# A fixed order of the items of every engine in place of a list scheduler's, and key sums by vector passes that transpose blocks

## The chip, the cores and the metric

The kernel runs on one core of a Trainium2 chip. The metric is the device time of one execution in microseconds (us); the time given for a kernel is the median of several runs. One execution is also taken by the hardware profiler, and all rows below are from that one.

## What is computed

For 64 heads (8 batches of 8) with 576 tokens of 64 channels, a linear attention with 256 features per token, and behind it a feed forward over all 4608 tokens:

```python
def phi(x):
    proj = x @ w_phi                                   # 64 -> 128
    proj = proj - max(abs(proj), axis=-1)
    return concat([exp(proj), exp(-proj)])             # 256 features
q_p, k_p = phi(q), phi(k)
kv  = k_p^T @ v                                        # 256 x 64 per head
z   = sum(k_p, over the tokens)                        # the key sums, 256 per head
out = (q_p @ kv) / (q_p @ z + 1e-6)
x   = out as 4608 x 512
y   = (max(x @ w_in, 0) ** 2) @ w_out                  # 512 -> 2048 -> 512
```

## The kernel before, in words

Two heads make a *pair*; there are 32 pairs, four of them per batch. The feed forward runs in 18 *chunks* of 256 tokens (c0 to c17), each in 8 *steps* (f0 to f7) of 256 hidden columns. A step is a first product (`gemm1`, L1051, 24 f16 matmuls into one PSUM bank `ph`), a scale and squares on ACT and DVE, and a second product (`gemm2`, L1088, 12 matmuls that add up in PSUM over the eight steps). Chunks c0 to c9 run so; the last eight run as four pairs of chunks with a saving scheme (L1233, "p1" and "p2", two parts of a first product for both chunks). The weights arrive as 64-bit words and are rebuilt on the chip: per block a load of 1 MB (L464), a size on ACT (L480), a low part on POOL (L483), a join on DVE (L487), a greatest value on ACT (L502, input weights only), a scale that PE spreads over the partitions (L422) and DVE rounds (L428 to L433), and two halves (L551 or L552, then L555) or three parts (L521, L331, L541).

The first six pairs are *early* (`early`): PE does all their work with transposes and sums of its own (k products L611 and L617, key times value L669, L674, key sums L702, turning L714, q products L730, L736, L764, L768, numerators L783, denominators L800). The other 26 pairs are *late* (`visit`, `late`): a visit is one block of PE work for three pairs at once (q products L884, then the next pair's k products L611, then columns L892, L617, L669, L674, then the last pair's numerators L904); POOL finds the greatest q projections (L982) and sums the denominators (L1003). In `keys` the late pairs' key features are folded by DVE adds (L650, L655, L660 over both heads) into one row, and in `late` that row is transposed in blocks of 32 x 32 (L966) and reduced (L967); it goes to DRAM and back (L971, L972) and is summed once more (L974). Tokens end in the `ring`, from which the feed forward reads (a multiply L835, a high part L857 or L864, a low part L860).

Nothing is issued while these lines run. Each is added as an item to a `Plan`: its engine (some have a second engine to choose), an assumed time, what it comes after and which buffers it uses. `order` is a list scheduler: it plays the items by assumed times, takes on each engine the ready item with the lowest rank (1108 ranks are set one by one, `RANKS`, read in `improve`), and returns them by start. They are then issued in that order, so each engine's stream is fixed when the program is built. Where the played PE stands idle for over 0.7 us before 125 us, matmuls of zeros (L1358) are put in.

Of the kernel before, what the change touches and what calls it, by code (L numbers as in the profile page):

```python
# [27 lines left out]
F = 128  # L28
# [21 lines left out]
STAY = 6.0  # L50
LATER = 2.0
BEHIND = 0.0
MOVED = 70.0
# [32 lines left out]
class Plan:  # L86
# [24 lines left out]
    def close(self):  # L111
# [18 lines left out]

        for (tag, n), mine in users.items():
            if tag in self.single:
                first = mine[0]
                first.after += [a for op in mine[1:] for a in op.after if a not in mine and not self.leads(first, a)]
        self.users = {key: len(mine) for key, mine in users.items()}

    def leads(self, first, op):
        seen, todo = set(), [op]
        while todo:
            x = todo.pop()  # L140
            if x is first:
                return True
            for a in x.after:
                if a.n not in seen:
                    seen.add(a.n)
                    todo.append(a)
        return False

    def improve(self):

        some = [op for op in self.ops if -50.0 < op.rank < MOVED]
        assert 2 * len(some) == len(RANKS)
        for n, op in enumerate(some):
            i, j = (DIGITS.index(x) for x in RANKS[2 * n:2 * n + 2])
            op.rank = (90 * i + j - 3000) * 0.05
        return self.order()

    def order(self):
        for op in self.ops:
            op.start = op.end = None  # L160
            op.next, op.left = [], 0
            op.after = [a for a in {id(a): a for a in op.after}.values() if a is not op]
            op.behind = [a for a in op.behind if a not in op.after and a is not op]
        for op in self.ops:
            for a in op.after + op.behind:
                a.next.append(op)
                op.left += 1
        free = dict.fromkeys(self.HOP, 0.0)
        waiting = {e: [] for e in self.HOP}
        ready = {e: [] for e in self.HOP}  # L170
        holder, open_at, parked = {}, {}, {}
# [3 lines left out]

        def alone(op):
            return [key for key in op.uses if key[0] in self.single]

        def release(op):
            least = max([open_at.get(tag, 0.0) for tag, n in alone(op) if holder.get(tag) != n] + [a.start + 0.001 for a in op.behind], default=0.0)  # L180
            for eng in op.ways:
                at = least
                for a in op.after:
                    at = max(at, a.there + (self.HOP[a.eng] if a.eng != eng or a.land else 0.0))
                second = eng != next(iter(op.ways))
                heapq.heappush(waiting[eng], (at + LATER * second, op.rank + BEHIND * second, op.n))

        def gone(n):
            return self.ops[n].start is not None

        for op in self.ops:
            if not op.left:
                release(op)
        done = 0
        while done < len(self.ops):
            best = None
            for e in self.HOP:
                while ready[e] and gone(ready[e][0][1]):
                    heapq.heappop(ready[e])
                while waiting[e] and gone(waiting[e][0][2]):  # L200
                    heapq.heappop(waiting[e])
                if not waiting[e] and not ready[e]:
                    continue
                t = free[e] if ready[e] else max(free[e], waiting[e][0][0])
                if best is None or t < best[0]:
                    best = t, e
# [42 lines left out]
            for x in op.next:  # L249
                x.left -= 1  # L250
                if not x.left:
                    release(x)
# [1189 lines left out]
```

## Time and profile before

| what | us |
|---|---|
| median of 3 runs (1019.26 to 1021.61) | 1020.16 |
| span of the profiled execution | 1018.5 |
| PE busy | 999.8 |
| DVE busy | 763.2 |
| ACT busy | 680.5 |
| POOL busy | 361.2 |

The span runs from the first to the last instruction; the runs' median lies 1.7 us above it. PE's granted clock was 0.998 of full speed over the span. PE's busy time counts matmuls, with those of zeros among them; weight loads are counted apart (694.6 us) and mostly lie beside the matmuls. A busy PE is not always a PE with useful work: a matmul's record includes its way through the array.

### The profile page before, as it was taken

How to read it: one execution, taken by the hardware profiler on the slowest of the kernel's cores; microseconds unless marked ns; L12 is line 12 of the kernel's file. 1: busy time of each engine (PE TensorE's matmuls, PEld its weight loads, DVE VectorE, ACT ScalarE, POOL GpSimd, SP SyncE). 2: the span in 40 equal slices, each digit the busy share in tenths (PEclk: the TensorE clock that was granted, in tenths of full speed). 3: DMA queues.
4: the chain of work that ended last, by engine and by line, in shares of the span. 5: the costliest groups of instructions: out<-in, count | busy, mean ns of one | idle time of the engine just before them, and what ended most of it. 6: DMA issues, size and time to landing. Idle time of an engine off the chain costs nothing.

```text
span 1018.5 us, 19261 instructions
## 1 busy us (share of the span) xinstructions
PE 999.8 (98%) x7632; PEld 694.6 (68%) x7713; DVE 763.2 (75%) x1221; ACT 680.5 (67%) x1206; POOL 361.2 (35%) x138
## 2 busy tenths in 40 slices
PE   8999999999999999999999999999999999999998
PEld 4657776776666667666767666666776767677675
DVE  5899878798878989777879888798888447343432
ACT  6989886777777787686777867776555445435444
POOL 2433356364456555475375646563000000000000
PEclk9999999999999999999999999999999999999999
DMA  9754323132322233233324212110002001000001
GB/s 355 282 186 135 122 81 94 39 110 73 85 60 81 75 93 93 60 82 81 107 80 111 83 48 69 41 41 22 13 2 83 1 1 49 14 1 21 22 1 42
DMA packets 94914, 77.34 MB, mean 76 GB/s; under 512 B 58088, under 2 KB 72424, under 8 KB 92776
## 3 DMA queue, kind: packets, MB, share of 16 engines
q1 hardware_dynamic: 94536, 75.59, 24.6%
q8 instruction: 60, 0.98, 0.4%
q10 hardware_dynamic: 288, 0.52, 0.1%
q14 instruction: 30, 0.25, 0.1%
HBM read 61.16 MB, written 14.78 MB: 75 GB/s over the span
## 4 chain that ended last, share of the span: by engine, by line
PE 90%; DVE 3%; DMA 3%; ACT 2%; issue 1%; SPq 0%; DVEq 0%; ACTq 0%
PE po L1088 27%; PE ph L1051 21%; PE pp L1233 7%; PE pz L669 4%; PE pv L1088 4%; PE pn L1088 4%; PE ph L1233 3%; PE pn L904 3%; PE pn L884 2%; PE pp L611 2%; PE pv L904 2%; PE pz L1233 2%; PE pz L674 1%; PE pv L669 1%; PE pz L892 1%
## 5 line engine op out<-in xcount | busy, mean ns | idle before, releaser
L1051 PE MATMUL ph<-ring,win 128*128 128x256 f16 x2064 | 240.4, 273 | 0.8 <-ACT r L1060 0.8
L1051 PEld LDWEIGHTS <-win 128*128 128x128 f16 x2064 | 195.3, 98 | 47.0 <-issue 24.8
L982 POOL PARTITION_ALL_REDUCE mx<-pt x52 | 121.6, 2339 | 122.7 <-ACT pt L335 84.3
L1088 PE MATMUL po<-wh,gh 128*128 128x512 f32 x448 | 143.8, 442 | 0.0
L1003 POOL PARTITION_ALL_REDUCE rb<-rb x26 | 96.5, 3712 | 112.0 <-DVE rb L1000 95.6
L1265 ACT ACTIVATE qe<-qe,cw 128x512 f32<-128x512 f32 x58 | 41.4, 715 | 112.5 <-DVE qe L1248 112.5
L1088 PE MATMUL po<-wl,gl 128*128 128x512 bf16 x448 | 115.1, 379 | 0.0
L331 DVE TENSOR_TENSOR gl<-r,gh 128x512 bf16<-128x512 f32 x86 | 87.5, 1018 | 31.7 <-ACT r L1070 30.7
L1003 POOL PARTITION_ALL_REDUCE ds<-ds x26 | 98.7, 3797 | 25.2 <-DVE ds L1000 24.5
L1088 PE MATMUL po<-wl,gh 128*128 128x512 bf16 x375 | 101.5, 379 | 4.9 <-issue 1.6
L1088 PEld LDWEIGHTS <-gl 128*128 128x128 bf16 x576 | 56.4, 98 | 68.0
L1088 PEld LDWEIGHTS po<-wh,gh 128*128 128x128 f32 x448 | 84.6, 189 | 25.9
L1248 DVE TENSOR_TENSOR qe<-pp,qe 128x512 f32<-128x512 f32 (+1 forms) x87 | 52.3, 602 | 61.3 <-PE pp L1233 59.5
L1060 ACT ACTIVATE r<-ph,cw 128x512 f32<-128x512 f32 x86 | 58.7, 683 | 51.0 <-PE ph L1051 49.3
L331 DVE TENSOR_TENSOR gl<-qe,gh 128x512 bf16<-128x512 f32 x58 | 40.1, 691 | 65.7 <-ACT qe L1070 65.6
L1088 PEld LDWEIGHTS <-gh 128*128 128x128 bf16 x576 | 52.3, 98 | 50.7 <-issue 8.9
L633 ACT ACTIVATE e<-e 128x512 f32<-128x512 f32 x64 | 40.0, 625 | 32.3 <-DVE e L630 32.3
L1233 PEld LDWEIGHTS <-win 128*128 128x128 f16 x522 | 48.8, 98 | 14.2 <-issue 7.8
L1068 ACT ACTIVATE gh<-r 128x512 fp32r<-128x512 f32 x86 | 54.1, 629 | 5.7 <-PE pv L1088 2.0
L1070 ACT ACTIVATE r<-r 128x512 f32<-128x512 f32 x86 | 54.3, 631 | 2.7
L650 DVE TENSOR_TENSOR es<-e 128x512 f32<-128x512 f32 x52 | 46.3, 890 | 4.5 <-ACT e L635 4.3
L669 PE MATMUL pz<-e,v 128*64 128x256 f32 x416 | 49.3, 379 | 0.0
(286 smaller groups left out, 1970.4 us busy)
## 6 DMA issues: line engine op xcount, KB each, us to landing
v<-in_vp_dram SPq DMA_DIRECT2D x32, 320.0 KB, 4.1
k<-in_kp_dram SPq DMA_DIRECT2D x32, 288.0 KB, 4.1
q<-in_qp_dram SPq DMA_DIRECT2D x32, 288.0 KB, 3.4
rb<-rd SPq DMA_DIRECT2D x64, 144.0 KB, 3.1
out_dram<-o SPq DMA_DIRECT2D x34, 256.0 KB, 2.1
td<-kvs SPq DMA_DIRECT2D x26, 128.0 KB, 2.6
kz<-td SPq DMA_DIRECT2D x26, 128.0 KB, 2.9
spill<-ring SPq DMA_DIRECT2D x6, 256.0 KB, 2.9
```

The lines of the kernel that those rows point to most:

```text
L331: eng.tensor_tensor(out=out_, in0=a, in1=b_, op=ALU.subtract)
L669: PE.matmul(out=to[64 * h:64 * h + 64, 0:256], lhsT=v_[p][:, t, h, :], rhs=e_[2 * p + h][:, t].rearrange("p s f -> p (s f)"), start=t == 0 ...
L904: PE.matmul(out=to[64 * h:64 * h + 64, :], lhsT=kz_[n][:, 128 * s_ + 64 * h:128 * s_ + 64 * h + 64], rhs=qe_[2 * n + h].rearrange("p (s x) ...
L982: o = P.add("POOL", par_us(S), lambda n=n, h=h: G.partition_all_reduce(mx_[n], pt_[p][:, h, :], channels=128, reduce_op=bass_isa.ReduceOp. ...
L1003: o = P.add("POOL", 3.6, lambda y=y: G.partition_all_reduce(y(), y(), channels=128, reduce_op=bass_isa.ReduceOp.add), [o], [home], R(RQ + ...
L1051: PE.matmul(out=ph[:, j, :], lhsT=win[w][:, t, 128 * ff:128 * ff + 128], rhs=at_ring(c, x, t), start=k == 0, stop=k == 3 * KT - 1)
L1060: o = P.add("ACT", act_us(512, 1), lambda: A.activation(out=r_[n], in_=ph_[bank], func=AF.Relu, scale=cw[:, f, 0:1]), [g1], [("ph", bank), ...
L1068: sq = P.add("ACT", act_us(512), lambda: A.activation(out=gh_[n], in_=r(), func=AF.Square), after, use + [("gh", n)], Q)
L1070: o = P.add("ACT", act_us(512), lambda: A.activation(out=r(), in_=r(), func=AF.Square), [sq], use, Q, other=[("DVE", 0.70, lambda: V.tenso ...
L1088: PE.matmul(out=bank(i), lhsT=x[:, j, 128 * i:128 * i + 128], rhs=w[:, j, :], start=turn + j + s == 0, stop=(turn, j, s) == (NFP - 1, 1, 2))
L1233: PE.matmul(out=to, lhsT=fl(x, *al)(k), rhs=fr(y, *ar)(k), start=n == 0, stop=n == 5)
L1248: V.tensor_tensor(out=to, in0=a, in1=b, op=ALU.add)
```

## The change

Four things change.

1. `order` no longer schedules. A text `ORDER` holds two characters for each of the 3139 items: the item's place in one list for all engines. A text `WAYS` holds one digit for each of the 558 items that may run on more than one engine: which one. The items are issued in that order. The assumed times (some of them edited) still decide where zeros are put in and nothing else. `RANKS` and `improve` go.
2. The late pairs' key sums: per head one DVE reduce over the whole 128 x 1024 features that transposes blocks of 32 x 32 on its way, and one of 128 x 256 for the tail, 3 passes per pair. Before there were 8 (three adds for each head, one transpose, one reduce). The result is 128 x 72 numbers rather than 128 x 16; it goes to DRAM and comes back by two DMAs rather than one, into columns 256 to 327 of `kz`.
3. In a visit the q products and the k products are items of their own and wait only for their own inputs; before they were one item that waited for the inputs of all three pairs, and columns and numerators waited likewise. The order may now put other work between them.
4. A second half of `close` goes, which had made the first user of a PSUM bank wait for the inputs of its later users.

The matmuls, the passes of the feed forward and the loads are the same in kind and number.

```diff
 class Plan:
     def order(self):
+        assert 2 * len(self.ops) == len(ORDER)
+        place = {}
+            i, j = (DIGITS.index(x) for x in ORDER[2 * op.n:2 * op.n + 2])
+            place[op.n] = 90 * i + j
+        several = [op for op in self.ops if len(op.ways) > 1]
+        for op, way in zip(several, WAYS, strict=True):
+            op.take(list(op.ways)[int(way)])
+        order = sorted(self.ops, key=lambda op: place[op.n])
 ...
-        return sorted(self.ops, key=lambda op: (op.start, op.n))
+        return order
 ...
     def keys(p, main, to, use, tail, to_tail, use_tail, rank):
-            o = P.add("DVE", dve_us(512), lambda n=n: V.tensor_tensor(
-                out=es_[p][:, 512:1024], in0=e_[n][:, 0:2].rearrange("p t s f -> p (t s f)"),
-                in1=e_[n][:, 2:4].rearrange("p t s f -> p (t s f)"), op=ALU.add),
 ...
+            def fold(src, col, k, after, use, rank):
+                sums[p].append(P.add("DVE", dve_us(256 * k), lambda: V.tensor_reduce(
+                    out=col(), in_=src().rearrange("p k (b x) -> p k b x", x=32), op=ALU.add, axis=AX.X, apply_transpose=True),
+                    [after], [use, ("z4", p)], rank))
 ...
     def visit(i):
+        if s is not None:
+            v.append(P.add("PE", 0.92, rows_q, [q_load[s]], [qn, qv, ("q", s)], R(0.0), mode=ROWS))
+        if k is not None:
+            v.append(P.add("PE", 0.92, rows_k, [k_load[k]], [pp, ("k", k)], R(0.0), mode=ROWS))
+        if v:
+            c = P.add("PE", us_c, columns, need, use_c, R(0.0), mode=COLS)
 ...
-            v3 = visited[0] = P.add("PE", 1.94, numerators, need + [c] + pt_of.get(s, [])[:2], use_n, R(0.0), mode=COLS)
+            v3 = visited[0] = P.add("PE", 2.04, numerators, [kz_of[n]] + qexp[n], use_n, R(0.0), mode=COLS)
 ...
     def late(p):
-        o = P.add("DVE", dve_us(512), lambda: V.transpose(es_[p][:, 512:1024], es_[p][:, 0:512]), sums[p], [("es", p)], R(RZ))
 ...
+        w = P.add("SP", 0.4, lambda: SP.dma_start(zd_[p], z4_[p]), sums[p], [("z4", p), ("zd", p)], R(RZ), land=1.9, xfer=0.1)
+        back.append(P.add("SP", 0.5, lambda: SP.dma_start(
+            kz_[p][:, 256:320].rearrange("p (a x) -> p a x", a=4),
+            zd_[p].rearrange("(a i) b x -> (i b) a x", a=4)[:, :, 0:16]), [w], [("zd", p), ("kz", p)], R(RZ), land=2.1, xfer=0.1))
+        back.append(P.add("SP", 0.5, lambda: SP.dma_start(
+            kz_[p][:, 320:328].rearrange("p (a s) -> p a s", a=4),
+            zd_[p].rearrange("(a i) b x -> (i b) a x", a=4)[:, :, 16:18]), [w], [("zd", p), ("kz", p)], R(RZ), land=2.1, xfer=0.2))
```

`ORDER` can be read without running anything: counting the items in the order in which the code adds them gives each its place, and the counts 3139 and 558 confirm the reading. PE's queue of the new order begins (p0 is pair 0, "k tail" L617, "k" L611, "q" L730, "turn q" L764, "kv" L669 and L674, "sums" L702, "flip" L714, "num" L783, "den" L800, "scale" L422):

```
zeros; q p0; k tail p0; k p0; q p1; turn q p0; k p1; k tail p1; kv p0; sums p0; scale batch 0; k p2; flip p0;
q tail p0; turn q p0; num p0; kv p1; k tail p2; sums p1; turn q p1; scale w0; flip p1; q p2; k p3; ...
... den p4; num p3; q tail p5; k p6 (of the first visit); flip p5; num p4; num p4; first product c0 f0; turn q p5;
columns p6; turn q p5; q p6; first product c0 f1; k p7; scale w3; first product c0 f2; num p5; num p5; den p5;
second product c0 f0; ...
```

The loads of the new order begin with w_phi, q p0, k p0, input weights f0, q p1, v p0, v p1, k p1, v p2, input weights f1, v p3, input weights f2, k p2, output weights f0, output weights f1, k p3.

## Rows read from the trace of the kernel before

**Rows 1.** Busy time by stretch: length, PE, weight loads, DVE, ACT, POOL (instructions); clock; DMA share, GB/s

```profile
0.00:82.80 82.80, 75.20 (x851) 46.83 (x854) 65.39 (x124) 69.61 (x131) 26.29 (x24) 0.98 0.71 257
125.00:700.00 575.00, 571.38 (x4434) 397.05 (x4475) 484.83 (x772) 421.95 (x778) 315.93 (x105) 1.00 0.28 76
700.00:1000.00 300.00, 296.83 (x1961) 210.69 (x1988) 170.99 (x268) 143.91 (x231) 4.96 (x2) 1.00 0.05 18
...
0.00:22.00 22.00, 17.25 (x160) 10.24 (x161) 12.85 (x29) 13.35 (x26) 3.72 (x9) 0.92 0.91 345
22.00:82.80 60.80, 57.95 (x691) 36.59 (x693) 52.53 (x96) 56.26 (x106) 22.57 (x16) 1.00 0.63 225
```

**Rows 2.** PE's waits from 125 us on: who for whom, us, times, longest

```profile
PE pp L1233 <- DVE qe L1248: 0.9, 1, 0.9
PE ph L1051 <- ACT r L1060: 0.8, 1, 0.8
```

**Rows 3.** Timeline around the first feed-forward matmul: start, us, engine, line, operation

```profile
79.61 0.77 ACT L857 ACTIVATE ring<-rb,cb 128x576 f16<-128x576 f32 x1
81.27 0.81 DVE L860 SCALAR_TENSOR_TENSOR ring<-rb,cb,ring 128x576 f16<-128x576 f32 x1
82.80 2.79 PE L1051 MATMUL ph<-ring,win 128*128 128x256 f16 x24
85.43 0.49 PE L714 MATMUL pv<-ident,kvs 128*128 128x128 f32 x3
85.76 0.61 PE L422 MATMUL pn<-ident,wm 128*128 128x128 f32 x4
86.30 1.16 PE L611 MATMUL pp<-wraw,k 64*128 64x128 f32 x16
...
95.42 0.44 PE L736 MATMUL pn<-wraw,q 128*64 128x128 f32 x4
95.69 1.14 PE L783 MATMUL pv<-qe,kz 128*64 128x288 f32 x8
```

**Rows 4.** Timeline, the first pass on loaded data of DVE and of ACT

```profile
5.63 0.29 DVE L637 TENSOR_REDUCE kmt<-pn 128x1 f32<-128x128 f32 x1 [4.12 <-PE pn L617]
...
6.28 0.31 ACT L643 ACTIVATE et<-et 128x128 f32<-128x128 f32 x1 [4.28 <-DVE et L640]
```

**Rows 5.** Groups of DVE and ACT in 0 to 82.8 us: busy us, mean ns of one

```profile
L835 DVE TENSOR_TENSOR rb<-n,rb 128x576 f32<-128x576 f32 x4 | 3.2, 789 | 0.0
...
L487 DVE SCALAR_TENSOR_TENSOR u<-u,raw0o 128x1024 int32<-128x1024 int32 x1 | 1.2, 1250 | 0.1
...
L551 ACT ACTIVATE win<-u,cw 128x1024 f16<-128x1024 f32 x3 | 3.4, 1141 | 0.0
L335 ACT ACTIVATE kvs<-pv 128x384 f32<-128x384 f32 x6 | 2.9, 490 | 0.4 <-PE pv L702 0.4
```

**Rows 6.** DMA issues by line: times issued, KB each, median us from issue to landing

```profile
raw5i<-in_w_in_dram SPq DMA_DIRECT2D x1, 1024.0 KB, 15.4
...
za<-zd SPq DMA_DIRECT2D x26, 8.0 KB, 1.8
```

**Rows 7.** Timeline, a small DVE pass beside a POOL pass

```profile
50.26 2.33 DVE L817 TENSOR_SCALAR den<-den 128x9 f32<-128x9 f32 x1
...
49.81 2.75 POOL L331 TENSOR_TENSOR wl<-u,wh 128x1024 bf16<-128x1024 f32 x1
```

**Rows 8.** Groups of DVE, whole span: first and last two of the five key-sum groups

```profile
L650 DVE TENSOR_TENSOR es<-e 128x512 f32<-128x512 f32 x52 | 46.3, 890 | 4.5 <-ACT e L635 4.3
...
L966 DVE STREAM_TRANSPOSE es<-es 128x512 f32<-128x512 f32 x26 | 18.4, 707 | 0.4
L967 DVE TENSOR_REDUCE z<-es 128x16 f32<-128x512 f32 x26 | 17.8, 683 | 0.5
```

**Rows 9.** Chain that ended last: a first product behind a second product, and behind a visit

```profile
295.91 2.64 PE ph L1051 x24
...
313.14 2.73 PE ph L1051 x24
```

More of the change, by code (lines that the diff above doesn't have):

```diff
@@ L129, in close @@
                 op.after.append(first)
[L131 to L134, printed above, removed]
         self.users = {key: len(mine) for key, mine in users.items()}
[L137 to L156, printed above, removed]
     def order(self):
+        assert 2 * len(self.ops) == len(ORDER)
+        place = {}
         for op in self.ops:
[L160 to L167, printed above, removed]
+            i, j = (DIGITS.index(x) for x in ORDER[2 * op.n:2 * op.n + 2])
[4 more added lines that the diff above has]
+        order = sorted(self.ops, key=lambda op: place[op.n])
         free = dict.fromkeys(self.HOP, 0.0)
-        waiting = {e: [] for e in self.HOP}
-        ready = {e: [] for e in self.HOP}
-        holder, open_at, parked = {}, {}, {}
+        holder, open_at = {}, {}
         mode, moved = WHOLE, 0.0
@@ L174, in order @@
         users = dict(self.users)
[L176 to L186, printed above, removed]
@@ new lines, in order @@
+        for op in order:
+            e, (us, _, lock) = op.eng, op.ways[op.eng]
+            op.start = max([free[e]] + [a.there + (self.HOP[a.eng] if a.eng != e or a.land else 0.0) for a in op.after if a is not op]
+                           + [a.start + 0.001 for a in op.behind if a is not op])
+            alone = [key for key in op.uses if key[0] in self.single]
+            for tag, n in alone:
+                assert holder.get(tag, n) == n
+                if tag not in holder:
+                    op.start = max(op.start, open_at.get(tag, 0.0))
+            op.end = op.start + us
@@ L1053, in gemm1 @@
                         k += 1
-        g1 = P.add("PE", 2.56, gemm1, after, [("ph", bank)], m)
+        g1 = P.add("PE", 2.61, gemm1, after, [("ph", bank)], m)
         if turn:
@@ L1375, in tile_kernel @@
         if free:
-            fills.append((t0, len(P.ops), lambda tag=free[0], n=n, count=int(0.6 * (t1 - t0) / 0.214): zeros(tag, n, count)))
+            fills.append((t0, lambda tag=free[0], n=n, count=int(0.6 * (t1 - t0) / 0.214): zeros(tag, n, count)))
     with tc.manual_schedule():
-        for _, _, fn in sorted([(op.start, op.n, op.fn) for op in order] + fills, key=lambda x: x[:2]):
-            fn()
+        for op in order:
+            while fills and fills[0][0] <= op.start:
+                fills.pop(0)[1]()
+            op.fn()
```

265 lines of the change are left out of this document (122 added, 143 removed).

## The prediction

> **What bounds the kernel now.** The busy time by stretch comes first. From 125 to 700 us PE is busy 571.38 of 575 us, from 700 to 1000 us 296.83 of 300, at a granted clock of 1.00, the higher of its two levels; DVE, next in line, is busy 484.83 of the 575 [rows 1]. So from the first feed-forward chunks on PE has work at every moment, and the list of PE's waits says the same: after 125 us only two exceed 0.2 us, one of 0.9 and one of 0.8 us [rows 2]. The timeline is read second, where this state begins. The first feed-forward matmul starts at 82.80 us. ACT's high part of pair 3's tokens, the last that chunk 0 needs, starts at 79.61, DVE's low part at 81.27 and ends at 82.08 [rows 3]; PE then finishes a numerator and starts the chunk. Before that point PE cannot be filled: it is busy 75.20 of 82.80 us, zeros included, while ACT has 69.61 us of work and DVE 65.39 [rows 1]. So the time is: when the first feed-forward matmul starts, plus PE's remaining work, plus a few waits, plus the end. PE's matmuls are the same after the change. What it can move is the start of the chunks, the two waits, and the cost of going from one kind of matmul to another. The runs' median lies 1.7 us above the profiled span (1020.16 against 1018.5), and I add that at the end.
>
> The words "fixed order" change nothing by themselves: each engine's stream was fixed when the program was built. Only which order it is, and the key sums, can act.
>
> **Part 1, the start of the chunks.** The new order puts more of PE's small work ahead of the first chunk: a flip, a scale, a k product, a q tail, a numerator and a short k tail, all of which now come just after it. By starts and lengths they are 0.33, 0.54, 1.0, 0.27 and 1.0 us [rows 3], with some 0.2 for the tail: 3.3 us. PE's remaining work is shorter by that, so the first chunk may start at 86.1 us (82.80 + 3.3) with nothing lost; each us earlier or later moves the end by one.
>
> When can it start? I count what the new order puts on ACT and DVE ahead of pair 3's ring parts, against what ran until 82.80 us.
>
> ACT: three more sizes, two more w_in halves and two more w_out parts, less one w_out part: six passes of 1024 columns at 1.14 us; one more ring copy (0.77); two more short exponentials (0.31 each); seven fewer PSUM copies at about 0.45 [rows 3 to 5]. That is 6.8 + 0.8 + 0.6 - 3.2 = +5.0 us, so 74.6. ACT's first exponential is at 6.28 us [rows 4] with 1.3 us of table load ahead of it, so without any idle time the high part ends at 6.3 + 74.6 - 1.3 = 79.6 and the chunk can start 0.9 us later, at 80.5.
>
> DVE: three more joins, two more w_in halves and two low parts of w_out (seven passes of 1.25, 8.7); eight PSUM copies that WAYS sends to DVE (3.6, priced as ACT's); one w_out high part (0.7), one weight scale (1.0), six key and query passes (2.5); less four multiplies (0.79 each, now on POOL), three short passes (1.2) and the one that was held up (2.2) [rows 5, 7 and 8]. That is +9.9, about +9.1 where neighbours overlap as they do now, so 74.5 us. From the first pass at 5.63 us [rows 4], with 0.7 of memsets before it, the floor is 79.4 us.
>
> Until now DVE idled 11.8 us between its first pass and the end of the low part (82.08 - 5.63 = 76.45, less 64.7), ACT 8.2. With all of DVE's idle time kept the chunk would start at 91.2; with none, at ACT's 80.5. These are the ends. I take half of DVE's idle time, 5.9 us, and so 85.3 us: 0.8 us are gained. Why half: the idle time is mostly there because inputs are missing. DVE is busy 12.85 us in the first 22 and idles 8.3 of the 60.8 us after [rows 1]. The third k load now stands behind three weight loads of 1 MB rather than five; one took 15.4 us to land, queued, at 345 GB/s [rows 1 and 6], 3 us of transfer each, so it comes 6 us sooner. The extra weight passes are also work to fill holes with. But the chain at the start (first loads, two exponentials per half, the turning of q) is as long as before, so the first 4 us of idle time stay, and ACT would have to run with only 4.8 us of idle time in place of 8.2.
>
> **Part 2, the key sums.** Five groups of DVE passes go, the first 46.3 us and the last 17.8 [rows 8], 155 us in all. Their replacement is not in the trace. The nearest rows are the reduce of 128 x 512 (683 ns) and the block transpose of the same size (707). If one pass does both at the pace of either, a head costs 1.4 and a tail 0.45: 52 x 1.4 + 26 x 0.45 = 84 us. If turning costs a pass of its own, 168 us. I take 84, since either row alone runs an element per cycle. Both ends leave DVE below 500 us of the 575 [rows 1], and PE waits for nothing there, so this is worth 0 to the end: the gain of 70 us lies off the path. The second DMA back adds 26 issues to SP, with the loads and denominators behind it; today's one lands in 1.8 us [rows 6]. What waits for it are the denominators and then the ring, and in the new order a chunk's first use comes over 30 us of PE work after its last numerators: price 0, and 1 us if a ring part once came late.
>
> **Part 3, the visits split, and PE's changes of kind.** After the first chunk matmul a count of the new order has 110 changes between row-split, column-split and whole matmuls, where the trace has 93. A first product behind a visit takes 2.73 us, behind a second product 2.64 [rows 9]: 0.09 for a change. 17 x 0.09 = +1.5 us.
>
> **Part 4, the waits on PE.** The 0.8 us are two first products back to back on the one bank `ph`; the 0.9 us are two p parts followed by two more with no second product between [rows 2]. The new order has neither neighbourhood anywhere: -1.7 us. What is late next: first to second product now stand at least 10 us apart in the order, columns to numerators at least 18, single second products (2.6 us) stand between p2 and the next p1 ten times. I see no wait of note but bound it by 0 and 1.5 us, and take 0.5. The end of the program is the same.
>
> **The sum.** 1018.5 - 0.8 + 1.5 - 1.7 + 0.5 = 1018.0 span, and with 1.7 a median of 1019.7.
>
> **The rivals.** *Faster:* the new order packs ACT and DVE to a quarter of DVE's idle time (3 us); first chunk at 82.4, -3.7, with -1.7 and +1.5 a median of about 1016.3. For it: inputs earlier, more work to choose from. Against it: ACT would have 1.9 us of idle time in the whole prelude, against 8.2. *Slower:* the weight work pulled forward delays pair 3, with DVE idle 9 us or more; first chunk at 89, +2.9, one of the two waits replaced, and the median is about 1024. It decides from 88 us on. For it speaks a hold-up in the rows: a DVE pass of nine columns took 2.33 us and ended when a POOL pass of 2.75 us with two inputs did [rows 7]; WAYS moves four more two-input multiplies to POOL just there. The Trainium skill, page "SBUF — State Buffer", section "SBUF: two separate sides", says that GpSimd and a VectorE pass with two SBUF inputs take one port pair exclusively for a whole instruction; the trace agrees in that one 2.33 us pass, and by that rule four multiplies of an estimated 1.4 us (2.5 us for 1024 columns) could each hold DVE once, 5.6 us, and the median would be 1025. Against it: three such POOL passes cost only one visible hold so far. *Split visits wait:* parts of visits, now apart, each find an input 0.2 us late; 26 of them make +5, about 1025. Against it stand the distances of part 4. *Nothing:* the order is only another of equal worth, 1020.2, which lies inside the forecast.
>
> **Chances.** Forecast, within 0.2% (about 2 us, what a measurement can tell from no change): 0.45, 1018.1 to 1022.2. Faster rival 0.33. Late prelude 0.17 and waiting visits 0.05, together 0.22 for slower. The range runs from 1015.5 (first chunk at 82, no new waits) to 1024.5 (at 89, with some).
>
> **What would show it.** The start of the first L1051 matmul against 86.1 us decides most; DVE's and ACT's busy time ahead of it should be near 74 us each. The key-sum passes should read near 1.3 us and DVE's total near 690 us. PE's waits after 125 us should list neither of the two. I am wrong if PE's time after the first chunk matmul differs by over 3 us from the 932.4 (1018.5 less 86.1) of the sum, or if PE is found idle behind a visit.

## The result, and the profile after

| | kernel before | changed kernel |
|---|---|---|
| median, us (runs, lowest to highest) | 1019.71 (4, 1018.42 to 1021.61) | 1025.59 (4, 1024.51 to 1026.08) |
| span of the profiled execution | 1018.5 | 1023.4 |
| first feed-forward matmul starts at | 82.80 | 88.48 |
| from there to the end of the span | 935.7 | 934.9 |
| DVE busy | 763.2 | 748.2 |
| ACT busy | 680.5 | 556.3 |

The ratio is 1.0053 (95%: 1.0040 to 1.0066): slower by 0.5%, where no change was forecast. The new order has 3.3 us more of PE's small work ahead of the first chunk, so its break-even was a start at 86.1 and a rest of 932.4 us. Both were missed, the start by 2.4 us and the rest by 2.5.

Busy time by stretch of the changed kernel (columns as in [rows 1]):

```profile
0.00:22.00 22.00, 18.10 (x176) 11.77 (x177) 13.66 (x33) 13.92 (x26) 4.11 (x9) 1.00 0.91 349
22.00:88.48 66.48, 60.31 (x723) 39.22 (x724) 63.07 (x111) 59.94 (x108) 33.84 (x23) 1.00 0.67 240
125.00:700.00 575.00, 574.13 (x4415) 393.18 (x4412) 445.04 (x747) 332.67 (x645) 299.24 (x103) 1.00 0.30 75
700.00:1000.00 300.00, 300.00 (x2010) 212.79 (x2009) 188.90 (x310) 115.94 (x194) 3.59 (x1) 1.00 0.06 20
```

Against [rows 1], DVE has 40 us less and ACT 89 us less work between 125 and 700 us, and PE is as full as before: what the change frees lies beside a PE that is busy anyway. Over the span DVE lost 15 us and not the 73 of the forecast (763.2 to 690): `WAYS` also sends DVE work that ACT did before, which has 124 us less. Ahead of the first chunk DVE is now busy 63.07 of 66.48 us from 22 us on.

The timeline around the start, to set beside [rows 3]: POOL multiplies pair 3's tokens (1.79 us; on DVE it took 0.79 [rows 5]), ACT and DVE write their two ring parts, the chunk follows.

```profile
84.76 1.79 POOL L748 TENSOR_TENSOR rb<-n,rb 128x576 f32<-128x576 f32 x1 [4.81 <-ACT n L255]
...
86.58 0.78 ACT L770 ACTIVATE ring<-rb,cb 128x576 f16<-128x576 f32 x1
...
87.55 0.81 DVE L773 SCALAR_TENSOR_TENSOR ring<-rb,cb,ring 128x576 f16<-128x576 f32 x1
...
88.48 2.78 PE L962 MATMUL ph<-ring,win 128*128 128x256 f16 x24
```

DVE passes held up beside POOL's weight passes, three of five such places ahead of the first chunk, and for comparison one pass that was not held, at 77.55 (timeline):

```profile
41.67 1.41 POOL L402 TENSOR_SCALAR raw3o<-raw3o 128x1024 int32<-128x1024 uint32 x1 [2.03 <-DMA raw3o<-in_w_out_dram]
...
42.02 1.09 DVE L730 TENSOR_SCALAR den<-den 128x9 f32<-128x9 f32 x1
...
67.17 1.15 POOL L402 TENSOR_SCALAR raw6i<-raw6i 128x1024 int32<-128x1024 uint32 x1 [1.96 <-DMA raw6i<-in_w_in_dram]
67.67 0.68 DVE L730 TENSOR_SCALAR den<-den 128x9 f32<-128x9 f32 x1
...
77.55 0.16 DVE L730 TENSOR_SCALAR den<-den 128x9 f32<-128x9 f32 x1
...
78.81 1.14 POOL L402 TENSOR_SCALAR raw5o<-raw5o 128x1024 int32<-128x1024 uint32 x1 [1.67 <-DMA raw5o<-in_w_out_dram]
79.17 0.80 DVE L348 TENSOR_SCALAR pw<-pw 128x2 int32<-128x2 int32 x1
```

A pass of nine columns takes 0.16 us alone and 1.09 or 0.68 beside a POOL pass, and each of the small held passes ends within 0.03 us of it. The five places (L474 0.72 us over its usual time, L730 0.92, 0.10 and 0.51, L348 0.56) make 2.8 us.

PE's waits from the first chunk on (columns as in [rows 2]):

```profile
PE pn L713 <- ACT n L255: 0.8, 1, 0.8
PE pp L530 <- DVE ds L911: 0.3, 1, 0.3
PE pv L817 <- ACT pt L255: 0.3, 1, 0.3
PE ph L962 <- DVE r L973: 0.3, 1, 0.3
```

The two waits of [rows 2] are gone; four others make 1.7 us. Around the second of them the step from second product to k product takes 3.13 us (timeline):

```profile
581.13 1.03 PE L999 MATMUL po<-wl,gh 128*128 128x512 bf16 x4
...
584.26 1.16 PE L530 MATMUL pp<-wraw,k 64*128 64x128 f32 x16 [0.30 <-DVE ds L911]
```

The new key-sum pass (group of DVE: busy us, mean ns), in place of the groups of [rows 8], and three steps of the chain as in [rows 9], a first product behind a visit, one behind a small scale product and one behind a second product:

```profile
L568 DVE TRANSPOSE_TENSOR_REDUCE z<-e 128x32 f32<-128x1024 f32 x52 | 63.9, 1230 | 0.0
```

```profile
304.82 2.73 PE ph L962 x24
...
310.43 2.62 PE ph L962 x24
...
315.70 2.64 PE ph L962 x24
```

### The profile page after: what moved, and what is told of

It is laid out like the page before. It is cut to its first block, busy times and chain, and to the rows that moved or that the text cites. A ratio compares the mean times of both kernels' runs of the same rounds, so it can differ in the third digit from the quotient of the medians.

```text
span 1023.4 us, 19287 instructions
## 1 busy us (share of the span) xinstructions
PE 1007.5 (98%) x7718; PEld 694.1 (68%) x7718; DVE 748.2 (73%) x1266; ACT 556.3 (54%) x1028; POOL 349.3 (34%) x141
## 4 chain that ended last, share of the span: by engine, by line
PE 86%; DVE 6%; DMA 4%; ACT 2%; issue 1%; SPq 1%; POOL 0%; DVEq 0%; POOLq 0%; ACTq 0%
PE po L999 28%; PE ph L962 21%; PE pp L1144 7%; PE pv L999 4%; PE pn L999 4%; PE pz L582 4%; PE ph L1144 4%; PE pn L817 3%; PE pn L796 2%; PE pp L530 2%; PE pv L817 2%; PE pz L1144 2%; DMA rb<-rd 1%; DVE u L406 1%; PE pz L587 1%; PE pz L805 1%
## 5 line engine op out<-in xcount | busy, mean ns | idle before, releaser
L893 POOL PARTITION_ALL_REDUCE mx<-pt x52 | 117.0, 2249 | 103.6 <-DVE qe L251 38.8
L999 PE MATMUL po<-wl,gh 128*128 128x512 bf16 x448 | 115.5, 380 | 0.0
L914 POOL PARTITION_ALL_REDUCE ds<-ds x26 | 95.9, 3688 | 18.5 <-DVE ds L911 11.7
L251 DVE TENSOR_TENSOR gl<-r,gh 128x512 bf16<-128x512 f32 x86 | 70.0, 816 | 4.5 <-ACT r L981 4.0
L971 ACT ACTIVATE r<-ph,cw 128x512 f32<-128x512 f32 x51 | 34.8, 683 | 56.4 <-PE ph L962 46.0
L979 ACT ACTIVATE gh<-qe 128x512 fp32r<-128x512 f32 x58 | 36.1, 625 | 52.2 <-PE po L999 42.3
L568 DVE TRANSPOSE_TENSOR_REDUCE z<-e 128x32 f32<-128x1024 f32 x52 | 63.9, 1230 | 0.0
L251 DVE TENSOR_TENSOR qe<-pt,mx 128x576 f32<-128x576 f32 x52 | 43.4, 835 | 16.8 <-POOL mx L893 12.5
L898 ACT ACTIVATE qe<-qe 128x576 f32<-128x576 f32 x52 | 35.2, 677 | 35.6 <-DVE qe L251 35.6
```

Source lines behind the costliest of these rows:

```text
L251: eng.tensor_tensor(out=out_, in0=a, in1=b_, op=ALU.subtract)
L568: sums[p].append(P.add("DVE", dve_us(256 * k), lambda: V.tensor_reduce(out=col(), in_=src().rearrange("p k (b x) -> p k b x", x=32), op=AL ...
L893: o = P.add("POOL", par_us(S), lambda n=n, h=h: G.partition_all_reduce(mx_[n], pt_[p][:, h, :], channels=128, reduce_op=bass_isa.ReduceOp. ...
L914: o = P.add("POOL", 3.6, lambda y=y: G.partition_all_reduce(y(), y(), channels=128, reduce_op=bass_isa.ReduceOp.add), [o], [home], R(RQ + ...
L979: sq = P.add("ACT", act_us(512), lambda: A.activation(out=gh_[n], in_=r(), func=AF.Square), after, use + [("gh", n)], Q)
L999: PE.matmul(out=bank(i), lhsT=x[:, j, 128 * i:128 * i + 128], rhs=w[:, j, :], start=turn + j + s == 0, stop=(turn, j, s) == (NFP - 1, 1, 2))
```

## The experiments

The ratios are to the kernel before, measured in the same comparison, with their 95% intervals. Names of items: `num`, `inv`, `mul`, `thigh` and `tlow` with a pair's number are its numerators, the inverse of its denominators, its ring multiply and its two ring parts; `g1 c0 f0` is the first feed-forward product. All kernels are the changed kernel with the edit shown.

### Is it the order or the key sums?

**1.** The old order with the new items.

```diff
-ORDER, WAYS: as in the changed kernel
+ORDER, WAYS: places and engines of the kernel before; fold p.h where its adds stood
```

> The changed kernel's items (one key-sum pass per head, the second DMA back, split row visits) in the order and on the engines of the kernel before; only the DMAs back of the key sums go behind the third k load. Theory, the order costs the 6 us: the first feed-forward matmul starts near 82.8 us as in the kernel before, and the time is that of the kernel before, within 1.5 us of its median in the same comparison. Rival, the new key sums or their added DMAs cost it: 3 us or more above the kernel before, with the first chunk late or with PE waits behind DVE.

Measured: ratio 1.0239 (1.0217 to 1.0260), first chunk at 83.22. The rival's price came, and PE behind DVE; the cause was in neither theory. The waits of DVE and of PE after the start:

```profile
DVE zc L885 <- DMA kz<-zd: 78.8, 25, 4.8
...
PE ph L962 <- ACT r L971: 11.2, 9, 2.7
```

DVE stands in 25 waits behind the way back of the key sums, 78.8 us in all, since they now land in `kz`, which is free only after the numerators of two pairs back; the scale pass of a chunk waits behind DVE, and PE behind that. The start itself is the old one.

**5.** The same with a tile of its own for the way back.

```diff
+    zk_ = tiles(sm, "zk", [128, 72], F32, 1, EARLY)
-            kz_[p][:, 256:320].rearrange("p (a x) -> p a x", a=4),
+            zk_[p][:, 0:64].rearrange("p (a x) -> p a x", a=4),
```

> As the first experiment (the changed kernel's items in the order and on the engines of the kernel before), but the key sums come back into a small tile of their own (72 columns, one buffer) and no longer into columns 256 to 327 of kz; with that, every item keeps the place it has in the kernel before. Theory: the 25 us of the first experiment came from VectorE standing behind that way back (its waits on DMA kz, 78.8 us in 25 waits, are in its trace), since kz is free only after the numerators two pairs back; they go, and the time is that of the kernel before within 1.5 us. Rival, the transposing passes or the second DMA themselves hold up the engines: 5 us or more above the kernel before.

Measured: 1.0036 (1.0022 to 1.0049), first chunk at 83.63. That lies between theory and rival. The waits behind the way back are gone, and every first product stands 0.8 to 1.5 us behind its like in the kernel before (0.8 at the first, 1.1 at the last). What is left: these 1.1 us, 0.8 of them from the start, and the end of the program. There the last two output DMAs took 2.81 us to issue; the second line is the changed kernel's:

```profile
1016.12 2.81 ACTq L1033 DMA_DIRECT2D out_dram<-o  x2
```

```profile
1019.67 1.03 ACTq L1032 DMA_DIRECT2D out_dram<-o  x2
```

**16.** To see whether that belongs to the key sums, one output copy near the end went from ACT to DVE.

```diff
-WAYS: "store c10.0" on ACT
+WAYS: "store c10.0" on DVE
```

> The fifth experiment (the kernel before's order and engines, the new key sums in their own tile) with one output copy near the end on DVE and not on ACT. In the fifth experiment's trace ACT took 2.33 us to issue the last but one output DMA, where every other kernel has 0.38. Theory, this is a stall of that program's instruction stream and no cost of the key sums: it goes when the stream shifts, and the time is 1 to 2 us above the kernel before (the first feed-forward matmul 0.8 us later). Rival, the key sums in the old order do cost 3 us: it stays at 3 to 4 us above.

Measured: 1.0029 (1.0017 to 1.0040), first chunk at 83.61. In its trace the two issues took 1.03 us again and the span was 1020.0, 1.5 above the kernel before. But its times lie in two groups, six from 1021.65 to 1022.09 and six from 1023.95 to 1025.74, and the profile is of the first. The mean granted clock was 0.999 to 1.000 in the first group and 0.997 or 0.998 in five of the second; where it was low there no trace shows. So the new key sums in the old order cost 1.5 us where they can be followed, and up to 4 by the interval.

**4.** The other side: each key-sum pass twice, in the new order.

```diff
+                def twice():
+                    for _ in range(2):
+                        V.tensor_reduce(...)
```

> The changed kernel with each key-sum pass executed twice, the second time over the same result: about 75 us more of DVE work (52 passes of 1.23 us and 26 of some 0.4). Theory, the key sums' length is off the path once the chunks run, and only those ahead of the first chunk matter: the few passes of the first pairs ahead of it cost up to 3 us at the start, and nothing behind it: 0 to 3 us above the changed kernel, all of it in the start of the first feed-forward matmul. Rival, DVE's load also costs while the chunks run: over 5 us, with PE waits behind DVE.

Measured: 1.0347 (1.0327 to 1.0366), 30 us above the changed kernel, of which 2 us lie in the start (90.47; in this trace the granted clock was 0.57 from 22 to 24 us and 0.58 from 24 to 26). The theory fell. PE's waits after the start, and busy time by stretch:

```profile
PE pp L530 <- DVE ds L913: 8.9, 6, 3.8
PE pp L530 <- DVE rb L913: 4.2, 2, 2.3
PE ph L964 <- DVE r L975: 3.3, 2, 3.0
...
```

```profile
125.00:700.00 575.00, 551.81 (x4191) 376.50 (x4234) 488.56 (x790) 320.04 (x623) 284.46 (x98) 0.99 0.29 74
```

DVE is busy 488.56 of 575 us, hardly more than the 484.83 of the kernel before [rows 1], which cost PE nothing there; here PE idles 23 us. So DVE's load alone doesn't tell. What fits is that each pass now ends later than the order was laid out for; whether the queue behind it or the later key sums themselves cost more was not separated.

### Where in the order?

**2.** The old order up to the first chunk, the new one behind it.

```diff
-items ahead of "g1 c0 f0": places of the changed kernel
+items ahead of "g1 c0 f0": places and engines of the kernel before; what is left over, then the changed kernel's
```

> The order of the kernel before up to the first feed-forward matmul, the changed kernel's order from there on. Theory, the late start is worth 2.4 us (88.48 less 86.1) and PE's time behind it 2.5 us: the first feed-forward matmul near 82.8 us, the time 2.5 to 3.5 us below the changed kernel, so 2 to 3.5 us above the kernel before. Rival, the rest of the order carries all of it: no more than 1 us below the changed kernel. Rival, only the start counts: the kernel before's time within 1 us.

Measured: 1.0173 (1.0159 to 1.0187). The weight passes that were left over piled up ahead of the first chunk, which started at 102.40: 13.9 us later than in the changed kernel, and the median is 13.4 us above its. The rest took 935.2 us, as there (934.9). So this run didn't undo the head; it shows that a us at the start is a us at the end.

**3.** The reverse.

```diff
-items behind "g1 c0 f0": places of the changed kernel
+items behind "g1 c0 f0": places and engines of the kernel before
```

> The changed kernel's order up to the first feed-forward matmul, the order of the kernel before from there on. Theory: the first feed-forward matmul at 88.5 us, the late start kept (2.4 us), the changes of kind and the new waits behind it gone: 2 to 3.5 us above the kernel before, and its two old waits of 0.9 and 0.8 us back. Rival, the start costs nothing because the later order makes up for it: within 1 us of the kernel before. Rival, the start is all: 5 us or more above it.

Measured: 1.0306 (1.0292 to 1.0320): again DVE behind the way back of the key sums (86.1 us in 25 waits), which neither theory nor rivals had. The first chunk stood at 87.28.

**8.** The same with the key sums' own tile.

```diff
+the edit of experiment 5 on top of experiment 3
```

> The changed kernel's order up to the first feed-forward matmul, the kernel before's from there on, with the key sums' own tile of 72 columns as above. Theory: the start stays late (88 us) and nothing else is lost: 2.4 us above the kernel before, within 1 us, and 2.5 to 4 us below the changed kernel. Rival, the later order of the kernel before doesn't fit a late start, whose work it finds moved: 5 us or more above the kernel before.

Measured: 1.0039 (1.0024 to 1.0053), first chunk at 91.17, and from there 933.7 us. The late start stays, 2.7 us later still than the changed kernel's (its granted clock was 0.63 and 0.52 from 22 to 26 us), and the rest is 1.2 us shorter. The median lies 4.1 us above the kernel before, where 2.4 within 1 was expected.

**10 and 11.** Near 180 us both orders have done the same items but for 18; there the parts were joined both ways (13 items of the second part of experiment 10 and 2 of the first part of 11 stand a little elsewhere).

```diff
+10: the kernel before's places for its first 712 items, then the changed kernel's
+11: the changed kernel's places for its first 706 items, then the kernel before's
```

> Both orders have done the same items but for 18 near 180 us. This kernel takes the order of the kernel before up to there and the changed kernel's from there on (key sums in their own tile). By the traces the changed kernel is 3.7 us behind at that point (181.30 against 177.6 for the same work) and loses 1.2 us in all the rest. Theory: 1.2 us from the rest and some 1 us from the new key sums ahead: 1.5 to 3 us above the kernel before, 2.5 to 4 us below the changed kernel. Rival, the rest of the order carries the loss: 4 us or more above the kernel before.

> The reverse: the changed kernel's order up to the same point, the order of the kernel before from there on. Theory: the 3.7 us of the start stay, the 1.2 us of the rest go: 3 to 4.5 us above the kernel before, 0.5 to 2 us below the changed kernel. Rival, the start costs little by itself: within 1.5 us of the kernel before.

Measured: experiment 10 1.0136 (1.0120 to 1.0151), with the first chunk at 82.86 and one wait of 7.4 us on PE at the joint, where DVE's queue came in another order than PE's; it decides nothing on the sum. From 216 us of the changed kernel on, each first product stands 6.7 us behind its like there, and 7.7 from 589 us on, behind a wait of 1.3 us that is 0.3 in the changed kernel: the rest of the new order adds little once it runs. Experiment 11: 1.0042 (1.0029 to 1.0054), first chunk at 89.16, the rest 934.1 us. As expected, what the changed kernel loses is mostly lost by 181 us; the time from the first chunk to the end is 0.8 us shorter, which the two overlapping intervals don't tell apart from nothing, and the two waits of [rows 2] are back in the trace (0.9 and 0.8 us).

**9.** Would the old order without these two waits be ahead?

```diff
-g1 c14 f6, g1 c13 f7, g2 c14 f5
+g1 c14 f6, g2 c14 f5, g1 c13 f7
-g2 c14 f4, p1 (15,16) f0, p2 (15,16) f0, p1 (15,16) f1
+p1 (15,16) f0, p2 (15,16) f0, g2 c14 f4, p1 (15,16) f1
```

> The kernel before's order with the new key sums in their own tile, as in the fifth experiment (3.3 us above the kernel before), with two items moved: a second product goes between the two first products that waited 0.8 us for each other, and one between the two pairs of p parts that waited 0.9 us. Theory, these two waits are worth what they show: 1.7 us below the fifth experiment, 1022.1; and since 1.8 us of the fifth experiment's 3.3 were a longer issue of its last output DMA (2.81 us where the other kernels have 1.03), which nothing in this change calls for, 1020.3 if that goes too: within 0.2% of the kernel before. Rival, the waits come back at the next item: as the fifth experiment, 1023.5 or more.

Measured: 1.0035 (1.0022 to 1.0047), no better than experiment 5. PE's waits from the first chunk on:

```profile
PE pp L1145 <- DVE qe L1160: 1.9, 1, 1.9
...
PE pp L531 <- DVE rb L912: 0.8, 1, 0.8
PE pz L1145 <- ACT qe L255: 0.6, 1, 0.6
...
```

The rival held: the waits came back at the next items, 3.3 us for the 1.7 that went. PE's last matmul starts 2.7 us later than in experiment 5, more than the list explains, while its last two output DMAs took 1.03 us to issue.

### What makes the start late?

**6.** Without the small held pass.

```diff
-            V.tensor_scalar(out=den_[p], in0=den_[p], scalar1=1e-6, scalar2=None, op0=ALU.add)
```

> The changed kernel without the pass that adds 1e-6 to the denominators (the addition is left out). This pass of nine columns takes 0.16 us where POOL rests and 1.09, 0.28 and 0.68 us in the three places ahead of the first chunk where it ends together with a POOL pass. Theory, these hold-ups delay DVE's unbroken queue: without them 2.2 us (1.5 of hold-ups and four passes of 0.17) leave DVE's queue ahead of the first chunk, the first feed-forward matmul starts 1.5 to 2.2 us sooner than 88.48, and the time is 1 to 2.5 us below the changed kernel. Rival, another chain (ACT, the way back of the denominators) is as late: less than 0.7 us sooner. Rival, the next DVE pass is held instead: the held time stays, less than 0.7 us sooner.

Measured: 1.0044 (1.0027 to 1.0062), first chunk at 88.05. Two things took the gain back in the trace. Other passes were held, the one below and two later ones for 0.9 us each (one of them by pair 3's multiply on POOL), and the granted clock fell to the lower level (0.50 is 1.2 GHz) after a stretch with PE busy 1.19 of 2 us:

```profile
33.66 1.14 POOL L402 TENSOR_SCALAR raw4i<-raw4i 128x1024 int32<-128x1024 uint32 x1
33.81 1.02 DVE L351 TENSOR_SCALAR cw<-pw 128x2 f32<-128x2 f32 x1
```

```profile
20.00:22.00 2.00, 1.19 (x15) 0.99 (x16) 1.44 (x7) 1.75 (x5) 1.12 (x1) 1.00 1.04 430
22.00:24.00 2.00, 2.00 (x15) 1.14 (x11) 0.69 (x1) 0.50 (x2) 0.17 (x1) 0.50 0.99 412
24.00:26.00 2.00, 1.94 (x10) 0.81 (x8) 1.82 (x4) 2.00 (x4) 0.94 (x1) 0.65 1.04 419
```

In experiment 11 the clock stayed at 1.00 behind 0.99 of 2 us, so that stretch alone doesn't decide it. Three of experiment 6's executions had a granted clock of 0.999 or 1.000 in the mean over the execution and took 1023.12 to 1023.60 us, some 2 us less than the changed kernel; the four at 0.996 to 0.998 took 1025.58 to 1027.86. That fits the theory's gain of 1 to 2.5 us where the clock held, but no trace of such an execution was kept.

**7.** Pair 3 first.

```diff
-cpn3.0 ... inv3;  kvmain5 ... num3.1;  num4.0, num4.1 ... g1 c0 f0;  mul3 on POOL
+inv3, cpn3.0;  num3.1, qmain5, kvmain5;  g1 c0 f0, num4.0, num4.1;  mul3 on DVE, ring parts ahead of the weight passes
```

> The changed kernel with only places in the order moved, ahead of the first chunk: on DVE pair 3's denominators go ahead of the copy that waits 1.35 us for POOL's multiply; on PE pair 3's second numerator goes ahead of pair 5's key-value product, and pair 4's numerators behind the first chunk matmul; pair 3's multiply goes from POOL to DVE, its ring parts ahead of the weight passes beside them. Theory, the order of these few items makes the late start: the first feed-forward matmul at 85.5 to 87 us instead of 88.48, with 2.3 us of PE's work moved behind it, so the time 0 to 1.5 us below the changed kernel. Rival, the whole prelude is bound by the amount of DVE's work: PE only idles elsewhere, no gain, or a loss.

Measured: 1.0071 (1.0054 to 1.0087), slower than the changed kernel; first chunk at 89.05 with 2.3 us of PE's work moved behind it. Pair 3's denominators came 0.4 us sooner only, and DVE now stood 1.15 us for their way back, with the weight passes queued behind it.

**12.** 8 us less of DVE's work.

```diff
-            o = P.add("DVE", dve_us(512), lambda n=n, x=x: V.tensor_reduce(
+            o = P.add("DVE", dve_us(512), lambda n=n, x=x: V.memset(km_[n], 0.0) if p < EARLY else V.tensor_reduce(
```

> The changed kernel with the maxima of the first six pairs' keys left out: the 12 reduces of 512 columns (0.69 us) and 6 of 128 (0.29) become memsets of 4 and 1 columns, so some 8 us of DVE's work ahead of the first chunk go and every wait and order stays. Theory, DVE's queue, which the chain of waits follows without a break from 24.6 to 68.4 us, sets the start: the first feed-forward matmul 3 us or more sooner than 88.48 and the time 3 us or more below the changed kernel, until ACT (59.9 us of work in 66.5) or PE binds. Rival, the way of pair 3's denominators (two DMAs of some 2 and 5 us, POOL's multiply of 1.8) or PE's own queue sets it: under 1 us.

Measured: 1.0057 (1.0045 to 1.0069), nothing gained; first chunk at 89.22. DVE has 59.82 us of work in 67.22, 3.2 less than in the changed kernel, and the start doesn't come sooner:

```profile
22.00:89.22 67.22, 61.94 (x739) 39.93 (x738) 59.82 (x113) 59.87 (x109) 36.60 (x24) 0.97 0.67 239
...
27.99 2.37 POOL L251 TENSOR_TENSOR wl<-u,wh 128x1024 bf16<-128x1024 f32 x1
...
28.15 3.28 DVE L406 SCALAR_TENSOR_TENSOR u<-u,raw2i 128x1024 int32<-128x1024 int32 x1
```

In the changed kernel the same two passes met the other way round:

```profile
26.70 1.31 DVE L406 SCALAR_TENSOR_TENSOR u<-u,raw2i 128x1024 int32<-128x1024 int32 x1
...
27.01 3.25 POOL L251 TENSOR_TENSOR wl<-u,wh 128x1024 bf16<-128x1024 f32 x1
```

Whichever starts first runs at its own pace (DVE 1.31 us, POOL 2.37) and the other waits for its end. The Trainium skill, page "SBUF — State Buffer", section "SBUF: two separate sides", says just this of GpSimd and a VectorE pass with two SBUF inputs or in a 2-port mode: the first to start has the shared port pair for the whole instruction. So a shift of these two starts against each other by 0.5 us cost DVE 2.0 us and gave POOL 0.9.

**13, 14 and 15.** The multiplies back on DVE, the copies back on ACT, and some of the work pulled forward put behind pair 3.

```diff
+13: WAYS: mul0, mul1, mul2, mul3 on DVE
+14: WAYS: cpkvs0, cpn0.0, cpkvs1, cpkz1, cpdn0, cpdn2, cpkz4, cpn3.0 on ACT
+15: lower3, lower4, cpn3.0 behind inv3;  val5b, kmax6.0, join6i behind tlow3.0
```

> The changed kernel with the four ring multiplies of pairs 0 to 3 back on DVE (0.79 us each), where the kernel before has them, and not on POOL (1.41 to 1.79). Theory, the amount of DVE's work sets the start: +3.2 us of DVE, less some 0.6 us of the shorter multiply of pair 3 and less waiting of DVE's copy behind POOL's multiply (1.35 us): the start 0 to 2 us later, the time no lower than the changed kernel's. Rival, POOL's two-input passes hold DVE or the chain up: 1 to 3 us below the changed kernel.

> The changed kernel with the eight PSUM copies ahead of the first chunk that went to DVE back on ACT: 3.6 us less of DVE's work, 3.6 us more of ACT's, which has 6.5 us of idle time between 22 and 88.48 us. Theory, DVE's queue sets the start: 1 to 3 us below the changed kernel, less where ACT then is late. Rival, ACT is as full as DVE: no gain or up to 2 us above it.

> The changed kernel with six DVE items moved in its order, none added: two low parts of w_out (1.2 us each) and the copy that waits 1.35 us for POOL go behind pair 3's denominators, and a join, a w_in half and a reduce go behind pair 3's ring part. Theory, what the new order puts on DVE ahead of pair 3 makes it late: denominators some 1.5 us sooner (den's DMA lands no sooner than 75.9), the first feed-forward matmul 0.5 to 2 us sooner, the time lower by as much. Rival, PE's own queue is as late (it is free at 88.1): under 0.4 us.

Measured: 1.0078 (1.0058 to 1.0097), 1.0067 (1.0055 to 1.0080) and 1.0088 (1.0075 to 1.0101), first chunks at 93.20, 89.85 and 91.91: none faster. Experiment 13 does not show a price of the multiplies: its two executions with a mean granted clock of 0.999 and 1.000 took 1025.35 and 1025.27 us, the changed kernel's time, and the four at 0.995 to 0.998 took 1029.00 to 1030.71; in its trace the clock was 0.56 and 0.58 from 22 to 26 us. For 14, with the clock at 1.00 in its trace, a full ACT fits; its interval overlaps the changed kernel's. 15, which adds no work, was expected to gain. There PE waited for an ACT copy of pair 5 (1.57 us), and pair 3's multiply came at 87.33:

```profile
85.60 1.19 PE L696 MATMUL pv<-qe,kz 128*64 128x288 f32 x8 [1.57 <-ACT kvs L255]
...
87.33 1.41 POOL L748 TENSOR_TENSOR rb<-n,rb 128x576 f32<-128x576 f32 x1 [7.13 <-ACT n L255]
```

**17 and 18.** Less of PE's work, alone and with experiment 12.

```diff
-            for t in range(5):
+            for t in range(4, 5):
```

> The changed kernel without 16 of the 20 matmuls of ones that sum each of the first six pairs' exponentials on PE (the sums are left incomplete): some 0.9 us per pair, 5 us of PE's work ahead of the first chunk, nothing taken from DVE, ACT or POOL. Theory, PE, DVE and ACT are equally full in the prelude, so that taking work from one alone brings little (8 us of DVE's work brought nothing): the time 0 to 2 us below the changed kernel. Rival, PE's own queue sets the start: 3 us or more below.

> Both at once: the maxima of the first six pairs' keys left out (8 us of DVE's work) and 16 of 20 matmuls of ones of each of these pairs (5 us of PE's). Theory, both queues are co-limiting: now 3 us or more come off, the first feed-forward matmul at 85.5 or sooner. Rival, ACT (59.9 us of work in 66.5), the third k load (landing at 21.7) or the way of the denominators sets it: no more than PE's relief alone gives, within 1 us.

Measured: 1.0055 (1.0038 to 1.0072) and 1.0047 (1.0032 to 1.0062), first chunks at 90.09 and 90.04: 5 us of PE's work less, in 18 also 8 us of DVE's, and no gain in the median that can be told. In both traces the granted clock fell to the lower level at 22 to 26 us, as in experiments 2, 4, 6, 8, 12 and 13, and not in the traces of the changed kernel or of experiments 3, 7, 11, 14 and 15; of experiment 18:

```profile
22.00:24.00 2.00, 2.00 (x19) 1.72 (x15) 0.00 (x0) 0.00 (x0) 0.00 (x0) 0.50 1.00 415
24.00:26.00 2.00, 1.51 (x8) 0.43 (x7) 0.95 (x3) 1.62 (x3) 1.11 (x1) 0.50 1.05 426
...
22.00:90.04 68.04, 58.40 (x577) 36.49 (x576) 60.23 (x109) 58.71 (x106) 33.88 (x23) 0.96 0.67 235
```

DVE and ACT are idle from 22 to 24 us while PE works at half speed, so part of what was taken away came back as longer matmuls. The executions fit that: 17 took 1023.93 and 1024.07 us at a mean clock of 0.998 and 1026.93 to 1028.12 at 0.995 to 0.997, 18 took 1023.89 at 1.000 and 1024.79 to 1026.48 at 0.997 or 0.998; the changed kernel's four, all at 1.000, took 1024.51 to 1026.08. So less of PE's work seems to gain some 1.5 us where the clock stays higher, half of what its rival asked. Less of DVE's alone gains nothing even there (experiment 12, one execution at 1.000: 1025.39). The clock does not sort all: experiment 14 took 1025.35 to 1028.36 at 1.000. Left untried are the third k load (a queue of 1 MB loads stands ahead of it) and ACT's amount of work.

## Why the prediction was wrong

**The step that failed is DVE's share of part 1.** It gave a start at 85.3; it was 88.48, past the 88 from which the slower rival was said to decide. That is 3.2 of the 5.4 us by which the span (1023.4) passed the forecast's 1018.0; 2.0 more are the new waits (part 4). Its terms, measured: the first DVE pass came at 6.70, not 5.63 (+1.1), because the new order begins with the q product of pair 0 and not with the short k tail. The work from there to the end of the low part was 76.1 us, not 73.8 (+2.3). The idle time was 5.6 us, where half of before's, 5.9, was taken. The mis-sized term is the hold-ups: the sum took the one held pass of [rows 7] off (2.2 us) as if it went with the old order, and put none in its place; 2.8 us came back at five others. Two small slips cancelled: 0.7 us of a pass behind the low part were counted as work ahead of it, and the 0.7 us between the low part's end and the chunk were left out.

The slower rival had the mechanism and the wrong partner: it priced POOL's four multiplies at 5.6 us, but in the changed kernel the partners are POOL's weight passes of one input, which stand in both kernels, and all held passes but one have one input too, as has the pass of [rows 7]. There the multiplies held nothing for over 0.1 us; in the traces of experiments 4, 6 and 12 one of them held a DVE join for 0.9 us.

**What the sum could not show.** A sum of DVE's work and idle time reads as if less work meant an earlier start. In the traces of experiments 12, 17 and 18 it was later by 0.7 to 1.6 us, with the clock at the lower level near 24 us. Moving a few items (7, 15), or engines (13, 14), made it later by 0.6 to 4.7 us, the most in 13, again with the lower clock. So the sum described this start and did not explain it. That the new head is late, whatever follows it, is shown: 87.28 to 91.17 (87.28 and 89.16 where the clock stayed up) in the traces of experiments 3, 6, 8 and 11, with the order ahead of it unchanged but for the one pass of 6, against 82.86 to 83.63 for the old head in 1, 5, 9, 10 and 16. Which of its parts makes it late stays open; the hold-ups' part is some 2 us by experiment 6's executions at the higher clock.

**Part 2, the key sums.** Their length was right: 1230 ns against 1.4 us for a head, 0.43 (26 passes) for a tail against 0.45. The Trainium skill, page "VectorE: DVE Perf Modes", section "The perf-mode tier table (the rule you actually need)", gives a reduce the plain rate alone and no faster mode; no run here shows it otherwise, with 1230 ns for 1024 columns beside 683 for 512 [rows 8], and the turning cost nothing on top. "Worth 0" held only at that length and in an order fitted to it. That both ends of the bound were worth 0 was wrong: at twice the 75 us of both the cost was 30 us (experiment 4), at a DVE load that the kernel before carried free of charge. And the price of 0 for the second DMA overlooked that its target `kz` is shared with the numerators: in an order not made for that the kernel took 25 us more (experiment 1), some 21 of which a tile of its own took away (experiment 5).

**Part 3, the changes of kind.** Right: a first product takes 2.63 us in front of a second product and 2.72 next to a visit, 0.09 for a change, 1.5 us for the 17 more.

**Part 4, the waits.** The two old ones went as forecast. The new ones are the 0.8 us of the list and four steps that are longer than their like by 0.4 to 0.5 us each (two steps from a visit's numerators on, 2.43 and 2.56 against 2.04 us; a second product, 3.13 against 2.75; a visit's columns, 3.13 against 2.76), the list's three waits of 0.3 among them: 2.5 in all, where 0.5 was taken and 1.5 was the bound. With part 3's 1.5 and the 1.7 that went that makes 2.3 of the rest's 2.5 us. The distances in PE's order said nothing of the queues on DVE and ACT between.

**The rivals.** "Late prelude" (89 us, about 1024, 0.17) has the numbers that came, 0.5 us sooner at the start and with some 2 us more behind it. In part that is luck: its condition, DVE idle for 9 us or more, did not come (5.6), and by the sum's own terms the lateness lies in the later first pass and in held work. The highest time of the range, 1024.5, stood for a start at 89 with some waits. "Split visits wait" showed in small: three of the four late steps stand at parts of visits, 1.3 us and not 5.

## What to carry to other kernels

In a fixed order for in-order queues a busy share is no slack: the same load of some 85% on one engine was free in the order made for it and came with 30 us in one made for less, so price an edit at what stands behind it in its queue. When a step removes a hold-up, ask which passes of the new order meet the same partner before taking the gain. When work is taken away to test a sum, look at the granted clock of every execution first: here it fell in some, with 2 to 5 us between executions of one program (experiments 6 and 13). And when a result is to come back in a tile that something else uses, the order is tied to that use; a small tile of its own (288 bytes of a partition) removed some 21 us here.

## What was not expected of the hardware

- The reduce that turns blocks of 32 x 32 runs in one pass: 1230 ns for 128 x 1024, where a transpose (707 ns) and a reduce (683 ns) of half the size stood before.
- Which of DVE and POOL is held depends on who starts first: 1.31 and 3.25 us, or 3.28 and 2.37, for the same two passes, decided by half a us.
- Two parts of a first product cost no more apart (1.98 and 2.63 us) than joined (4.60).
- One program took 2.33 us rather than 0.38 for an output DMA's issue on ACT near its end (experiment 5); with one instruction of ACT moved to DVE it was gone.
